# Forward to backward in a transformer block's decode kernel: the M products of head 30, the transposes of w3 and three weight loads are put in another place

## The chip, the core and the metric

The kernel runs on one core of a Trainium2 chip. A core has five engines that run side by side and wait for each other through semaphores: TensorE (PE, with its weight loads as PEld) multiplies matrices into PSUM, VectorE (DVE) and ScalarE (ACT) work element by element, GpSimd (POOL) and SyncE (SP) here issue transfers. Sixteen DMA engines move data between HBM and the on-chip memory. The metric is the device time of one execution in microseconds (us); lower is better. "Span" is the time from the first to the last instruction in the profiled execution.

## What is computed

One token goes through an adaptive-layer-norm block (attention over a cache of 8192 keys in 32 heads of width 192, then an MLP), and then the gradients of all inputs are formed. Cut to what matters:

```python
# B = 1, Sq = 1, D = 640, 32 heads, Sk = 8192, Dh = 192, F = 1536
def _A_ref(x, k, v, wq, wo):
    q = (x @ wq) as 32 heads
    p = softmax(einsum('bhqd,bhkd->bhqk', q, k) * Dh ** -0.5)
    return einsum('bhqk,bhkd->bhqd', p, v) as one row @ wo

def _B_ref(x, w1, w2, w3, w4):
    ...
    x1 = x + hs                      # hs is 0 for a single token
    return x1 + gelu(layernorm(x1) @ w3) @ w4

sa, ca, ga, sb, cb, gb = (silu(c) @ w_mod) in six parts
h = layernorm(x) * (1 + ca) + sa
x = x + ga * _A_ref(h, k_cache, v_cache, wq, wo)
h = layernorm(x) * (1 + cb) + sb
x = x + gb * _B_ref(h, w1, w2, w3, w4)
# returned: x, and the gradients of x, k_cache, v_cache, wq, wo, w3, w4, c and w_mod
```

The caches are 100.7 MB each; they are read, and their gradients (of the same size) are written.

## The kernel before

**Forward loop.** It runs over heads 0 to 30 (`for i in range(H1)`, H1 = 31) with three heads in flight: the scores of head i, softmax and scaling of V for head i−1, the end of head i−2. K and V come in halves of 1.57 MB (`load_k`, `load_v`) into five K buffers and three V buffers. Scores are products on DVE (`dot_mul`), summed by TensorE through the identity matrix. Each V half gives two quarters of V scaled by the exponentials ("vs", `scale_v`: some rows on DVE at L350, the others on ACT at L357, one ACTIVATE for each of up to 16 rows). For each quarter `m_quarter` adds K^T · vs to the head's matrix M (16 products at L372 for the first 128 columns of K, 16 at L377 for the other 64). M is kept, because the backward gets the gradient of q from it. The head's output row comes from a third set of products.

**The crossing.** After the loop comes straight-line code for the last two heads. Head 31 has no M; its output row, and that of head 30, come from `o_rows` (L392, 64 products each). Then: the output rows are divided by their sums (`pair_sums` L437 and L439, `pair_o` L443 to L448), multiplied with wo (`pair_ao` L455) and added into x1 (L651); layer norm 1, h_b, layer norm 2 (`g_layernorm`, a generator that is stepped with `next`, so that other work can be written between its steps; each mean is a product at L123); u = n2 · w3 (L783); gelu and its derivative; d_g, the gradient at the gelu's output, by twelve reductions of w4 on DVE (`dg_part`, L472); du; d_n2 from the transposed w3 (L834); two layer norms backward (`layernorm_bwd`); dao; and do, the gradient at the heads' outputs (`do_mm` L762, written to do_r at L765), the first operand of the backward loop.

Between these steps the code has other work: M of head 30 in quarters (`m_units` gives a quarter as three functions: the first 8 products of L372, the other 8, the 16 of L377; they are run by `f()` or `pe.pop(0)()`), the scaling of V for these quarters, the transposes of w3 (`w3t`, L725, with a copy from PSUM each, L726), gelu(u) · w4 (`h2_mm`, L822), the transposes of wo (`do_t`, L746), `mp_out` and `m_add` (M out of PSUM, L408, L410, L422), `e_rows` and `e_rows_out` (the exponentials transposed and stored to DRAM, L426 to L432; `load_er` at L704 loads them again for the backward).

**Loads of the crossing, in SP's order.** At i = 29 the loop issues three of w4's twelve row blocks into `w4b` (L560), at i = 30 the last pair's wo (L214), then the last V half of head 31, `load_v(H1, 1, KY)`. After it come the other nine blocks of w4 (L612), four fifths of w3 into the K buffer KX (L631) and the last fifth (L632).

**Backward loop.** It runs over 64 half heads. Each loads a V half, forms dP = V · do (L855 on DVE, L864 on PE, L314), dS, dK (L880) and dV (L875 on PE, L876 on ACT) and stores both; "side jobs" (weight gradients, q's gradient) are put between by a planner of slots.

**Order.** Within the crossing and the backward the order on PE, DVE, ACT and SP is that of the code (`manual_schedule`); POOL's order is that of its issues. Buffers come from pools: a tile is reused when its last reader is done, and where a pool is closed, its memory goes to later pools. The backward's pool `bst` is opened after the crossing's `vs` and `ft` are closed.

## Time and profile before

| | |
|---|---|
| times of the runs | 1434.04, 1435.51, 1438.58 us; median 1435.51 |
| the profiled execution | 1433.26 us, its span 1431.5 us |
| PE, DVE, ACT busy | 1105.0, 1104.2, 871.5 us (77%, 77%, 61% of the span) |
| moved | 569.38 MB by DMA; HBM read 340.95 MB, written 226.43 MB |
| mean granted TensorE clock | 0.768 |
| forward loop, crossing, backward | to about 533 us; 533 to about 594; from there to the end |

Busy shares are averages over stages with different limits. The page's slices divide the span into forty stretches of 35.8 us; a digit is a busy share in tenths, "PEclk" the TensorE clock that was granted (9 is full speed). In the rows in order of time the columns are: start in us, duration in us, engine and line, the operation, output and input tile, shapes and count; in brackets stands how long the engine had been idle before, and what ended that.

### The profile page before, as it was taken

The numbers are of one execution on the slowest core, as the hardware profiler recorded it, in microseconds if no ns is written. First come the engines' busy times: TensorE is split into PE (matmuls) and PEld (weight loads), VectorE is DVE, ScalarE is ACT, GpSimd is POOL, SyncE is SP. The second block draws the span as 40 slices with busy tenths as digits, with TensorE's granted clock in tenths as the row PEclk, the third lists the DMA queues.
The fourth block names the chain that finished last, engine by engine and source line by source line (L and its number), as shares of the span: only waits on it lengthen the run. The fifth ranks groups of instructions, "written<-read, shape, count | busy, mean of one in ns | idle before, by whom it ended". The sixth has DMA issues, their size and how long they took to land.

```text
span 1431.5 us, 30396 instructions
## 1 busy us (share of the span) xinstructions
PE 1105.0 (77%) x12744; PEld 790.1 (55%) x12744; DVE 1104.2 (77%) x1410; ACT 871.5 (61%) x1953; POOL 145.6 (10%) x254
## 2 busy tenths in 40 slices
PE   3988889999999998767757677677777777666864
...
PEclk9999999999999998766667575666655555556565
DMA  9999999999999995499999999999999999999998
GB/s 374 391 397 418 415 417 417 412 422 411 420 408 413 418 415 211 164 385 428 422 399 425 427 408 421 416 425 403 425 418 425 402 422 414 358 385 382 422 404 372
DMA packets 77417, 569.38 MB, mean 398 GB/s; under 512 B 8766, under 2 KB 26510, under 8 KB 36958
## 3 DMA queue, kind: packets, MB, share of 16 engines
...
q10 hardware_dynamic: 20, 0.00, 0.0%
HBM read 340.95 MB, written 226.43 MB: 396 GB/s over the span
## 4 chain that ended last, share of the span: by engine, by line
PE 26%; DVE 12%; DMA 8%; ACT 8%; issue 4%; POOL 1%; ACTq 0%; POOLq 0%; DVEq 0%; SPq 0%
PE dot_ps L864 17%; DVE pq L855 6%; ACT KB L876 6%; DMA wo_st<-in_A_wo_dram 4%; PE wT_ps L746 3%; PE dv_ps L875 3%; DMA stg<-in_A_wq_dram 2%; ACT wT L747 2%; DMA out_dram<-wo_st 2%; DVE dP L314 2%; DVE KB L880 1%; DMA out_dram<-stg 1%; PE do_ps L762 1%; DVE dq_junk L984 1%; DVE dS L1156 0%
## 5 line engine op out<-in xcount | busy, mean ns | idle before, releaser
L876 ACT CAST KB<-dv_ps 128x768 bf16<-128x768 f32 x512 | 376.3, 815 | 146.9 <-PE dv_ps L875 146.5
L864 PE MATMUL dot_ps<-pq,ident_bf 128*128 128x256 bf16 x1536 | 317.2, 388 | 50.2 <-DVE pq L855 50.1
L357 ACT ACTIVATE vs<-VB,Ef 128x192 bf16<-128x192 bf16 x872 | 314.9, 447 | 0.0
L864 PEld LDWEIGHTS <-ident_bf 128*128 128x128 bf16 x1536 | 198.5, 133 | 146.2 <-issue 77.4
L875 PE MATMUL dv_ps<-do_r,er_b 1*128 1x192 bf16 x2048 | 173.5, 309 | 131.1 <-ACT KB L876 129.9
L300 DVE TENSOR_TENSOR prod<-KB,qs_bc 128x6144 bf16<-128x6144 bf16 x62 | 207.9, 3353 | 30.0 <-DMA KB<-in_A_k_cache_dram 23.0
L880 DVE TENSOR_TENSOR KB<-qs_bc,dS 128x3072 bf16<-128x3072 bf16 x128 | 223.8, 1749 | 4.5 <-DMA out_dram<-KB 4.2
L855 DVE TENSOR_TENSOR pq<-VB,do_r 128x3072 bf16<-128x3072 bf16 x126 | 220.3, 1749 | 0.0
L372 PE MATMUL mp<-vs,KB 128*128 128x193 bf16 x1984 | 191.3, 249 | 4.3 <-ACT vs L357 2.8
L747 ACT COPY wT<-wT_ps 128x1024 bf16<-128x1024 bf16 x84 | 81.0, 964 | 185.4 <-PE wT_ps L746 185.4
L875 PEld LDWEIGHTS <-er_b 1*128 1x128 bf16 x2048 | 65.7, 102 | 223.2 <-issue 220.4
L372 PEld LDWEIGHTS <-KB 128*128 128x128 bf16 x1984 | 171.2, 98 | 13.6 <-DMA KB<-in_A_k_cache_dram 4.7
L310 PE MATMUL half_ps<-prod,ident_bf 128*128 128x256 bf16 x744 | 95.1, 279 | 45.8 <-DVE prod L304 45.4
L314 DVE TENSOR_REDUCE dP<-dot_ps 128x32 f32<-128x512 f32 x64 | 44.0, 688 | 109.8 <-PE dot_ps L864 109.8
L350 DVE TENSOR_TENSOR vs<-VB,E 128x1728 bf16<-128x1728 bf16 (+1 forms) x122 | 127.1, 1062 | 0.3 <-ACT vs L357 0.3
L304 DVE TENSOR_TENSOR prod<-prod 128x3072 bf16<-128x3072 bf16 x62 | 108.7, 1753 | 1.0
L310 PEld LDWEIGHTS <-ident_bf 128*128 128x128 bf16 x744 | 72.8, 99 | 64.1 <-issue 55.0
L377 PE MATMUL mp<-vs,KB 128*64 128x193 bf16 x1984 | 108.0, 252 | 0.0
L377 PEld LDWEIGHTS <-KB 128*64 128x64 bf16 x1984 | 80.8, 111 | 19.8 <-issue 19.7
L337 ACT ACTIVATE E<-S_h,negm 128x256 bf16<-128x256 f32 x31 | 15.8, 508 | 116.0 <-DVE negm L498 113.7
L704 POOL DMA_DIRECT2D er_b<-eT_d x64 | 37.3, 583 | 476.1 <-PE dv_ps L875 474.3
L432 POOL DMA_DIRECT2D eT_d<-er x16 | 8.8, 548 | 560.1 <-ACT vs L348 519.7
...
## 6 DMA issues: line engine op xcount, KB each, us to landing
...
VB<-in_A_v_cache_dram SPq DMA_DIRECT2D x123, 1536.0 KB, 11.6
...
```

Of the source, the lines that this page charges most:

```text
L300: V_.tensor_tensor(out=prod, in0=src, in1=vec[:, None, :].to_broadcast([P, JH, DH]), op=ALU.mult)
L310: T_.matmul(ps, lhsT=ident_bf, rhs=prod[:, :, k : k + TF], start=(k == 0), stop=(k == w - TF))
L350: V_.tensor_tensor(out=vs[:, 0:n, 0:DH].rearrange("p j (a b) -> p j a b", b=4), in0=v[:, v0 : v0 + n, :].rearrange("p j (a b) -> p j a b", ...
L357: A_.activation(out=vs[:, k, 0:DH], in_=v[:, v0 + k, :], func=ACT.Copy, scale=Ef[:, j0 + k : j0 + k + 1])
L372: T_.matmul(mp[:, 0:MW], lhsT=kb[:, j0 + k, 0:P], rhs=vs[:, k, 0:MW], start=(q == 0 and k == 0), stop=(z and k == JQ - 1), skip_group_chec ...
L377: T_.matmul(mp[p0 : p0 + 64, MO : MO + MW], lhsT=kb[:, j0 + k, P:DH], rhs=vs[:, k, 0:MW], start=False, stop=(z and k >= JQ - 2), skip_grou ...
L747: A_.copy(out=wT[:, x0 * P : (x0 + n) * P], in_=tp[:, 0 : n * P])
L855: V_.tensor_tensor(out=pq[:, q], in0=v_l[s][:, q * JQ : (q + 1) * JQ, :], in1=do_of(ht(s)[0])[:, None, :].to_broadcast([P, JQ, DH]), op=AL ...
L864: T_.matmul(ps[:, q * JQ : (q + 1) * JQ, :], lhsT=ident_bf, rhs=pq[:, q, :, k : k + TS], start=(k == 0), stop=(k == DH - TS), skip_group_c ...
L875: T_.matmul(ps[:, b, k * DH : (k + 1) * DH], lhsT=er[p0 : p0 + 1, 2 * m + k, :], rhs=doh[p0 : p0 + 1, :], start=True, stop=True)
L876: A_.copy(out=dV4[:, 2 * q : 2 * q + 2, m * PW : (m + 1) * PW], in_=ps[:, :, 0:PW])
L880: V_.tensor_tensor(out=dK[:, lo:hi, :].rearrange("p j (a b) -> p j a b", b=4), in0=qh.rearrange("p (a b) -> p a b", b=4)[:, None, :, :].to ...
```

## The change

In the loop, the loads of `w4b` at i = 29 and of the last wo at i = 30 go; both are issued after the last V half. In the crossing, the pair sums of heads 28 and 29 are taken ahead of head 30's V scaling; both `o_rows` follow each other; the four quarters of M are run in pieces of 8 or 16 products, each behind one of the chain's products on PE (quarter 0 around the output projection, quarter 1 in layer norm 1, quarter 2 in layer norm 2, quarter 3 among the transposes of w3). The scaling of quarters 0 and 2 is ACT's, that of 1 and 3 DVE's in halves of 8 rows (`vs_dve`). The last pair's o2 is made directly from the sums (`rm`). The large w3 load is issued behind quarter 1, which reads the buffer it goes to. `g_layernorm` can write a bf16 copy directly. w3's transposes, u, gelu, du, h2 and dn are moved into the crossing's pools: the transposes go to two `vs` buffers and KC in place of KC, `stg` and `w4b`, and use the PSUM of the score trees. The gelu's derivative is written with fewer steps behind the exponential. Both transposes of the last wo stand around dn and go to `w4b`; `mp_out` and `m_add` of head 30 come last.

(The lines of the crossing are indented less here than in the code.)

```diff
 def g_layernorm(x, name, res, n_bf=None):
...
+        if n_bf is not None:
+            V_.tensor_scalar(out=n_bf, in0=xc, scalar1=r[:, 0:1], scalar2=None, op0=ALU.mult)
...
-                if i % 2 == 0 and i > 0:
+                if i % 2 == 0 and 0 < i < H1 - 1:
                     wo_l[i // 2] = load_wo(i // 2)
...
-                if i == H1 - 2:
-                    nc.sync.dma_start(out=w4b[:, 0 : 3 * D].rearrange("p (a r) -> p a r", a=3), in_=w4v[:, 0:3, :])
...
+    def new_vs(q):
+        vs = vsp.tile([P, JQ, VW], BF16, name="vs")
+        A_.copy(out=vs[:, :, DH:VW], in_=E4[:, q * JQ : (q + 1) * JQ, :])
+        return vs
+    def vs_dve(vs, q, lo, hi):
+        j0, v0 = q * JQ, (q % 2) * JQ
+        V_.tensor_tensor(
+            out=vs[:, lo:hi, 0:DH].rearrange("p j (a b) -> p j a b", b=4),
+            in0=vy[q // 2][:, v0 + lo : v0 + hi, :].rearrange("p j (a b) -> p j a b", b=4),
+            in1=E4[:, j0 + lo : j0 + hi, None, :].to_broadcast([P, hi - lo, DH // 4, 4]),
+            op=ALU.mult,
+        )
+    def vs_act(vs, q, lo, hi):
+        j0, v0 = q * JQ, (q % 2) * JQ
+        for k in range(lo, hi):
+            A_.activation(out=vs[:, k, 0:DH], in_=vy[q // 2][:, v0 + k, :], func=ACT.Copy, scale=Ef[:, j0 + k : j0 + k + 1])
...
     x["v"].append(load_v(H1, 1, KY))
+    wo_l[TL] = load_wo(TL)
+    nc.sync.dma_start(out=w4b[:, 0 : 3 * D].rearrange("p (a r) -> p a r", a=3), in_=w4v[:, 0:3, :])
     negm = neg_max(mx)
     E4, Ef = softmax(H1 - 1, y["S"], negm)
     score_q(0, 1, d0)
     mt = m_out(H1 - 2, z["mp"], z["op"], os_)
-    op_y = psO.tile([P, 256], FP32, name="op")
-    o_rows(H1 - 1, vy, op_y)
-    vs0 = scale_v(0, vy[0], E4, Ef, 0)
-    mp = psM.tile([P, 512], FP32, name="mp")
+    po = pair_sums(os_.pop(TL - 1))
+    vs0 = new_vs(0)
+    vs_act(vs0, 0, 0, JQ)
     score_q(1, 0, d1)
     score_q(1, 1, d1)
-    vs1 = scale_v(1, vy[0], E4, Ef, JQ)
-    dot_sum(d0, x["S"][:, 0:JH])
-    for f in m_units(0, ky[0], vs0, mp):
-        f()
-    dot_sum(d1, x["S"][:, JH:J])
-    mx = row_max(x["S"])
-    po = pair_sums(os_.pop(TL - 1))
-    o_out(H1 - 1, op_y, os_)
     w4a = pp.tile([P, 9, D], BF16, name="w4a", tag="prod")
     nc.sync.dma_start(out=w4a, in_=w4v[:, 3:12, :])
     w4r = lambda a: w4b[:, a * D : (a + 1) * D] if a < 3 else w4a[:, a - 3, :]
-    for f in m_units(1, ky[0], vs1, mp):
-        f()
+    o2 = pair_o(TL - 1, po)
+    dot_sum(d0, x["S"][:, 0:JH])
+    mp = psM.tile([P, 512], FP32, name="mp")
+    pe = m_units(0, ky[0], vs0, mp)
+    pe.pop(0)()
+    dot_sum(d1, x["S"][:, JH:J])
+    mx = row_max(x["S"])
+    es0 = tcol(1, "es")
+    V_.reduce_sum(out=es0, in_=E_all[:, H1 - 1, :], axis=AX.X)
+    oy, zy = os_head(H1 - 1, os_)
+    ox, zx = os_head(H1, os_)
+    os2 = os_.pop(TL)
+    vs1 = new_vs(1)
+    A_.activation(out=zy, in_=es0, func=ACT.Copy, scale=32.0)
+    vs2 = new_vs(2)
     negm = neg_max(mx)
     A_.activation(out=E_all[:, H1, :], in_=x["S"], func=ACT.Exp, bias=negm[:, 0:1], scale=1.0)
+    op_y = psO.tile([P, 256], FP32, name="op")
+    o_rows(H1 - 1, vy, op_y)
+    vs_dve(vs1, 1, 0, JQ // 2)
+    es1 = tcol(1, "es")
+    V_.reduce_sum(out=es1, in_=E_all[:, H1, :], axis=AX.X)
+    vs_act(vs2, 2, 0, 1)
+    A_.activation(out=zx, in_=es1, func=ACT.Copy, scale=32.0)
+    A_.copy(out=oy, in_=op_y[:, 0:DH])
+    vs_dve(vs1, 1, JQ // 2, JQ)
     op_x = psO.tile([P, 256], FP32, name="op")
     o_rows(H1, x["v"], op_x)
-    vs2 = scale_v(2, vy[1], E4, Ef, JQ)
-    o2 = pair_o(TL - 1, po)
+    vs_act(vs2, 2, 1, 4)
     m_add(H1 - 2, z["mp"], mt)
-    vs3_ = []
-    vs3g = g_scale_v(3, vy[1], E4, Ef, vs3_, 0)
-    for _ in range(4):
-        next(vs3g)
-    ps_ao = pair_ao(o2, wo_l.pop(TL - 1))
-    V_.tensor_copy(out=AO[:, :, 2 * TL - 2 : 2 * TL], in_=ps_ao)
+    A_.copy(out=ox, in_=op_x[:, 0:DH])
+    ps_ao = pair_ao(o2, wo_l.pop(TL - 1), psB, "b")
     w3d = B_w3.rearrange("(i p) n -> p i n", p=P)
     w3_4 = wst.tile([P, F], BF16, name="w3_4", tag="wo")
-    nc.sync.dma_start(out=flat(KX)[:, 0 : 4 * F].rearrange("p (i n) -> p i n", i=4), in_=w3d[:, 0:4, :])
     nc.sync.dma_start(out=w3_4, in_=w3d[:, 4, :])
-    o_out(H1, op_x, os_)
+    po = psS.tile([P, 8], FP32, name="po", tag="s")
+    T_.matmul(po[:, 4:6], lhsT=c32, rhs=os2[:, 2 * DH : 2 * DH + 2], start=True, stop=True)
+    V_.tensor_copy(out=AO[:, :, 2 * TL - 2 : 2 * TL], in_=ps_ao)
+    V_.reciprocal(out=rinv[:, 2 * TL : 2 * TL + 2], in_=po[:, 4:6])
+    rm = tcol(2, "rm")
+    V_.tensor_tensor(out=rm, in0=omask[:, 0, :], in1=rinv[:, 2 * TL : 2 * TL + 2], op=ALU.mult)
+    for k in range(3):
+        T_.matmul(po[:, k : k + 1], lhsT=os2[:, k : 2 * DH : 3], rhs=c32[:, 0:1], start=True, stop=True)
+    vs_act(vs2, 2, 4, 8)
     aoP = tcol(ND, "aoP")
     V_.reduce_sum(out=aoP, in_=AO[:, :, 0 : 2 * TL], axis=AX.X)
     xP = tcol(ND, "xP")
     V_.tensor_tensor(out=xP, in0=ga, in1=aoP, op=ALU.mult)
     V_.tensor_tensor(out=xP, in0=xP, in1=x_c, op=ALU.add)
-    pe = m_units(2, ky[1], vs2, mp)
     pe.pop(0)()
-    po = pair_sums(os_.pop(TL))
-    dg_part(2)
-    o2 = pair_o(TL, po)
+    o2 = ft.tile([P, 3, 2], BF16, name="o2")
+    V_.tensor_tensor(out=o2, in0=po[:, 0:3, None].to_broadcast([P, 3, 2]), in1=rm[:, None, :].to_broadcast([P, 3, 2]), op=ALU.mult)
...
+    ps_ao = pair_ao(o2, wo_l[TL], psB, "b")
     pe.pop(0)()
-    ps_ao = pair_ao(o2, wo_l[TL], psB, "b")
-    for _ in vs3g:
-        pass
+    vs_act(vs2, 2, 8, JQ)
     aoN = tcol(ND, "aoN")
     V_.reduce_sum(out=aoN, in_=ps_ao, axis=AX.X)
     V_.tensor_tensor(out=x1, in0=ga, in1=aoN, op=ALU.mult)
...
     g = g_layernorm(x1, "ln1", res)
     next(g)
     V_.tensor_copy(out=AO[:, :, 2 * TL : 2 * TL + 2], in_=ps_ao)
+    pe = m_units(1, ky[0], vs1, mp)
     pe.pop(0)()
-    dg_part(1)
+    er_ps = e_rows(TL - 1, psB, "b")
     next(g)
-    pe = m_units(3, ky[1], vs3_[0], mp)
+    vs3 = new_vs(3)
+    vs_dve(vs3, 3, 0, JQ // 2)
     pe.pop(0)()
+    next(g)
+    e_rows_out(TL - 1, er_ps)
     pe.pop(0)()
-    dg_part(1)
-    next(g)
-    dg_part(1)
+    nc.sync.dma_start(out=flat(KX)[:, 0 : 4 * F].rearrange("p (i n) -> p i n", i=4), in_=w3d[:, 0:4, :])
+    vs_dve(vs3, 3, JQ // 2, JQ)
     next(g, None)
     n1, r1 = res.pop()
     V_.scalar_tensor_tensor(out=h_b, in0=cb, scalar=1.0, in1=n1, op0=ALU.add, op1=ALU.mult)
     V_.tensor_tensor(out=h_b, in0=h_b, in1=sb, op=ALU.add)
-    g2 = g_layernorm(h_b, "ln2", res)
-    next(g2)
-    pe.pop(0)()
-    dg_part(1)
-    mt = mp_out(H1 - 1, mp)
-    e_rows_out(TL - 1, e_rows(TL - 1, psB, "b"))
-    e_rows_out(TL, e_rows(TL, psB, "b"))
+    n2_bf = tcol(ND, "n2_bf", BF16)
+    g2 = g_layernorm(h_b, "ln2", res, n2_bf)
     next(g2)
     dg_part(1)
+    pe = m_units(2, ky[1], vs2, mp)
+    pe.pop(0)()
+    er_ps = e_rows(TL, psB, "b")
+    next(g2)
+    dg_part(1)
+    pe.pop(0)()
+    pe.pop(0)()
+    e_rows_out(TL, er_ps)
+    next(g2)
+    dg_part(1)
+    T0, T1 = (vsp.tile([P, JQ, VW], BF16, name="vs").rearrange("p j d -> p (j d)") for _ in range(2))
+    w3v = [flat(KX)[:, k * F : (k + 1) * F] for k in range(4)] + [w3_4]
+    w3Tv = [h[:, a * D : (a + 1) * D] for h in (T0, T1, flat(KC)) for a in range(4)]
+    def w3t_gen():
+        for a in range(NF):
+            tp = psR.tile([P, 1024], BF16, name="w3T_ps", tag="dot_ps")
+            for k in range(ND):
+                T_.transpose(out=tp[:, k * P : (k + 1) * P], in_=w3v[k][:, a * P : (a + 1) * P], identity=ident_bf)
+            A_.copy(out=w3Tv[a], in_=tp[:, 0:D])
+            yield
+    w3t_it = w3t_gen()
+    def w3t(n):
+        for _ in range(n):
+            next(w3t_it, None)
+    pe = m_units(3, ky[1], vs3, mp)
+    pe.pop(0)()
+    w3t(2)
+    next(g2, None)
+    n2, r2 = res.pop()
+    ups = psS.tile([P, NF], FP32, name="u_ps", tag="s")
+    for a in range(NF):
+        for k in range(ND):
+            T_.matmul(ups[:, a : a + 1], lhsT=w3v[k][:, a * P : (a + 1) * P], rhs=n2_bf[:, k : k + 1], start=(k == 0), stop=(k == ND - 1))
+    dg_part(2)
...
+    V_.tensor_copy(out=u, in_=ups)
+    V_.scalar_tensor_tensor(out=k2, in0=u, scalar=GELU_K1, in1=u, op0=ALU.mult, op1=ALU.mult)
+    V_.scalar_tensor_tensor(out=w_, in0=k2, scalar=1.0, in1=u, op0=ALU.add, op1=ALU.mult)
+    A_.activation(out=w_, in_=w_, func=ACT.Exp, scale=-2.0 * GELU_K0)
+    V_.tensor_scalar(out=e1, in0=k2, scalar1=6.0 * GELU_K0, scalar2=2.0 * GELU_K0, op0=ALU.mult, op1=ALU.add)
+    V_.tensor_tensor(out=e1, in0=e1, in1=u, op=ALU.mult)
+    w3t(2)
+    pe.pop(0)()
+    w3t(2)
+    pe.pop(0)()
+    V_.tensor_scalar(out=w_, in0=w_, scalar1=1.0, scalar2=None, op0=ALU.add)
+    V_.reciprocal(out=s_, in_=w_)
+    V_.tensor_tensor(out=g_, in0=s_, in1=u, op=ALU.mult)
+    g_bf = col(NF, "g_bf", BF16)
+    V_.tensor_copy(out=g_bf, in_=g_)
+    V_.scalar_tensor_tensor(out=t_, in0=s_, scalar=-1.0, in1=e1, op0=ALU.add, op1=ALU.mult)
+    V_.scalar_tensor_tensor(out=t_, in0=t_, scalar=-1.0, in1=s_, op0=ALU.add, op1=ALU.mult)
+    dg_part(NF)
+    du_bf = col(NF, "du_bf", BF16)
+    V_.scalar_tensor_tensor(out=du_bf, in0=t_, scalar=-1.0, in1=d_g, op0=ALU.mult, op1=ALU.mult)
+    V_.scalar_tensor_tensor(out=du, in0=t_, scalar=-1.0, in1=d_g, op0=ALU.mult, op1=ALU.mult)
...
+    w3t(2)
+    h2_mm(0, 2)
+    w3t(2)
+    h2_mm(2, 4)
+    w3t(2)
+    h2_mm(4, ND)
+    dw4_dve(flat(KX), 0, 0, 4)
...
+    def do_t(t, x0):
+        if x0 == 0:
+            woT[t] = w4b[:, 0 : 3 * D] if t == TL else bst.tile([P, 15 * P], BF16, name="wT", tag="wT")
+        w = wo_l[t]
+        transposed(x0, lambda a, b: [(0, P, w[:, a, b * P : (b + 1) * P])], 3, woT[t])
+    do_t(TL, 0)
+    dn_ps = psS.tile([P, ND], FP32, name="dn_ps", tag="s")
+    for k in range(ND):
+        for a in range(NF):
+            T_.matmul(dn_ps[:, k : k + 1], lhsT=w3Tv[a][:, k * P : (k + 1) * P], rhs=du_bf[:, a : a + 1], start=(a == 0), stop=(a == NF - 1))
+    d_n2 = tcol(ND, "d_n2")
+    V_.tensor_copy(out=d_n2, in_=dn_ps)
+    do_t(TL, 8)
+    mt = mp_out(H1 - 1, mp)
     m_add(H1 - 1, mp, mt)
...
-    w3Tv = [flat(KC)[:, a * D : (a + 1) * D] for a in range(9)] + [stg0[:, 0:D], stg0[:, D : 2 * D], w4b[:, 5 * D : 6 * D]]
...
-    w3t(1)()
-    next(g2)
-    dg_part(1)
-    next(g2, None)
-    n2, r2 = res.pop()
-    n2_bf = tcol(ND, "n2_bf", BF16)
-    V_.tensor_copy(out=n2_bf, in_=n2)
-    w3t(2)()
...
-    w3t(2)()
-    dg_part(2)
...
-    h2_mm(0, 2)
-    w3t(1)()
-    h2_mm(2, 4)
-    w3t(NF)()
-    h2_mm(4, ND)
-    dw4_dve(flat(KX), 0, 0, 4)
-    do_t(TL, 0)
-    dn_ps = psS.tile([P, ND], FP32, name="dn_ps", tag="s")
-    for k in range(ND):
-        for a in range(NF):
-            T_.matmul(dn_ps[:, k : k + 1], lhsT=w3Tv[a][:, k * P : (k + 1) * P], rhs=du_bf[:, a : a + 1], start=(a == 0), stop=(a == NF - 1))
     wo_l[TL - 1] = load_wo(TL - 1)
     er_l = {0: load_er(0), 1: load_er(1)}
-    d_n2 = tcol(ND, "d_n2")
-    V_.tensor_copy(out=d_n2, in_=dn_ps)
-    layernorm_bwd(d_n2, n2, r2, dbo, d_sb, "lb2", lambda: (do_t(TL, 8), dw4_dve(flat(KX), 0, 4, 5)))
+    layernorm_bwd(d_n2, n2, r2, dbo, d_sb, "lb2", lambda: dw4_dve(flat(KX), 0, 4, 5))
```

## The prediction

> **What bounds the kernel now.** I read the page's slices first, then one table of stretches, then the rows in order of time around the crossing from forward to backward.
>
> ```profile
> PE   3988889999999998767757677677777777666864
> PEclk9999999999999998766667575666655555556565
> DMA  9999999999999995499999999999999999999998
> GB/s 374 391 397 418 415 417 417 412 422 411 420 408 413 418 415 211 164 385 428 422 399 425 427 408 421 416 425 403 425 418 425 402 422 414 358 385 382 422 404 372
> ```
>
> Transfers fill both halves. They thin out only in slices 15 and 16 (537 to 608 us): 211 and 164 GB/s against some 415. There nothing is left to load and nothing is ready to store, so a chain of small steps sets the time, and a microsecond cut from it starts the whole backward a microsecond earlier.
>
> ```profile
> core 0: us, PE busy (x) PEld busy (x) DVE busy (x) ACT busy (x) POOL busy (x), PEclk, DMA share, GB/s
> 546.00:550.00 4.00, 4.00 (x48) 3.69 (x46) 3.06 (x8) 0.92 (x6) 0.00 (x0) 1.00 0.92 303
> 554.00:558.00 4.00, 2.61 (x32) 2.40 (x32) 3.21 (x14) 4.00 (x12) 0.00 (x0) 0.96 0.99 392
> 558.00:562.00 4.00, 4.00 (x32) 3.58 (x33) 3.28 (x14) 0.60 (x3) 0.00 (x0) 0.50 0.03 10
> 574.00:578.00 4.00, 4.00 (x87) 4.00 (x85) 1.61 (x6) 2.69 (x5) 0.00 (x0) 0.50 0.07 10
> ```
>
> Columns: window, its length, busy time per engine, granted clock, DMA share, GB/s. DMA is idle from 558 on, the TensorE clock is halved from there, and no engine is busy throughout: it is latency. The links, in order:
>
> ```profile
> 540.33 3.43 DVE L570 TENSOR_TENSOR pb<-KB,qs_bc 128x3072 bf16<-128x3072 bf16 x2 [3.09 <-DMA KB<-in_A_k_cache_dram]
> 543.68 1.75 DVE L350 TENSOR_TENSOR vs<-VB,E 128x3072 bf16<-128x3072 bf16 x1
> 549.08 0.20 ACT L404 ACTIVATE osb<-es 128x1 f32<-128x1 f32 x1 [3.28 <-PE po L439]
> 549.39 0.35 ACT L617 ACTIVATE E_all<-S_h,negm 128x64 bf16<-128x64 f32 x1
> 551.19 0.38 SPq L631 DMA_DIRECT2D KB<-in_B_w_dram  x1
> 554.04 0.82 DVE L472 CUSTOM_DVE_ANT_0 w4b<-w4b 128x640 bf16<-128x640 bf16 x1
> 557.51 0.17 DVE L651 TENSOR_TENSOR x<-x,xP 128x5 f32<-128x5 f32 x1
> 567.93 0.17 DVE L778 CAST n_bf<-ln_n 128x5 bf16<-128x5 f32 x1
> 569.93 0.17 DVE L788 COPY u<-u_ps 128x12 f32<-128x12 f32 x1 [0.23 <-PE u_ps L783]
> 574.10 0.17 DVE L808 CAST du_bf<-du 128x12 bf16<-128x12 f32 x1
> 579.66 0.16 DVE L839 COPY d_n<-dn_ps 128x5 f32<-128x5 f32 x1 [2.50 <-PE dn_ps L834]
> 585.26 0.42 ACT L765 ACTIVATE do_r<-do_ps,rinv 128x192 bf16<-128x192 f32 x1 [2.75 <-PE do_ps L762]
> ```
>
> The last K half lands at 540.33; the last exponential is at 549.39, x1 at 557.51, the second layer norm at 567.93, u at 569.93, du at 574.10, d_n2 at 579.66, the backward's first operand do_r at 585.26: 45 us in which little is moved.
>
> **The change, step by step.** Each line gives the end of a link before, and worked out for after.
>
> *Loads.* wo (0.49 MB) and the first part of w4 (0.49 MB) go behind V. The queue is full there; wo's landing followed K's by 1.16 us (540.21, 541.37), so K lands about 1.2 earlier (539.1), and the last half of V, 2.4 earlier, near 546.5. SP only issues in another order, nothing is queued behind a new wait.
>
> *Scores to exponential.* Before, both score sums stood behind the 1.75 us scaling at 543.68, and ACT waited until 549.08 for L439, queued on PE behind 16+16 M products. Both leave. What remains: two products 3.43, tree 1.47, sum 0.69, maximum 0.22, mx 0.49, negm 0.29, exponential 0.35, seven hand-overs at 0.04: 7.2. It ends at 546.3 instead of 549.74. Gain 3.4.
>
> *Output rows to x1.* Two L392 groups of 64 (1.50 each) run back to back, the second on V at 546.5: end 548.8 instead of 552.59. Then copy 0.30, sums 0.38 and 1.18, o2 0.17, ao 0.51, three DVE steps 0.6, hand-overs 0.3: 3.4. Before it was 5.1, with two L472 reductions (0.86 from start to start) ahead of o2. x1 ends at 552.3 instead of 557.68. Gain 5.4.
>
> *Two layer norms.* On PE an M block of 8 (half of L372's 1.51 per 16: 0.75 to 0.84) now stands behind each link, where whole quarters stood at half clock (2.75 and 1.50). A block of 8 lies beside the small DVE and ACT steps (0.7), the rest of 16 (0.86) beside Ln, Exp and what follows. Chain of the two: four means at 0.56, their sums 0.16, and 0.23+0.17, 0.29+0.20, 0.23 twice, h_b 0.34, hand-overs: 6.9. n2 at 559.2 instead of 568.10. The four half scalings of 1536 are not in the trace: at most 1.05 (L350 at 1728 columns), at least 0.84 (half of 1.68 back to back); 0.95 taken, in DVE's gaps. The second er copy waits on ACT for the first one's store (before: 3.45 from issue to landing) ahead of Ln: up to 1 us, hidden by the next step.
>
> *w3, the new wait.* Its 1.57 MB are issued behind the rest of M quarter 1, at 555.9 instead of 551.19. L214 at 576.90, alone on the queue, took 3.3 for 0.49 MB, of which 1.16 is transfer: 2.1 fixed. w3 then takes 2.1+3.7 = 5.8, bounds 3.7 (nothing fixed) and 9.8 (the V loads' median in this stretch under load); the queue is empty, so 5.8, landing 561.7. The link waits 2.5 for it. Ten transposes 0.7, 60 u products 1.74, copy: u at 564.4 instead of 570.1. Gain 5.7.
>
> *gelu and the w4 reductions.* Of twelve L472 only five are done by then; seven follow at 0.86: 6.0 after 2.0 of gelu steps, so du_bf is at 572.4 instead of 574.27. DVE has become the end here; beside it ACT needs 12 copies at 0.69 = 8.3 from 562.3 on (571 to 573), and PE its transposes, 24 M products and h2 (8 to 9 us at full clock). The four gelu steps saved (0.2 each) hide under this. Gain 1.9.
>
> *dn.* Before, PE came to dn 3.6 after du, held by transposes and h2 (577.83). Now these lie beside the seven reductions: dn 572.8 to 574.7, d_n2 4.9 earlier.
>
> *To do_r.* The layer norms' backward stays, 4.5. m_add (0.35) and its wait for two ACT copies (0.64), behind two wT copies (1.01 and 0.91), now stand between them on DVE: 0.4, at most 1.0. er's loads wait for that m_add: issued at 577.3 instead of 572.28, 1.9 to land, 579.2 against do_r at 580.6: 1.4 of cover, and PE's first dv_groups, c_ps and tree queue behind it if it goes.
>
> Sum: 4.9 − 0.4 = 4.5 us earlier. The backward does the same work behind it, so the shift carries to the end. Against this execution's own 1433.26 (span 1431.5 and 1.8 around it): 1428.8. It lies 2.25 below the median of the runs shown, 1435.51, which gives 1431.0 as the median to expect.
>
> **The clock.** The grant comes in steps of 3.4 us at 1.00 or 0.50: 0.96 over 554 to 558, where PE was busy 2.61 of 4 us, then 0.50. The sum has full clock up to w3's wait and a mix after.
> [...]
>
> **Rivals.**
> 1. *Half clock from w3's wait to the end of dn* (chance 0.17). For it: transposes and one-column products at 574 to 578 kept PE busy 4.00 of 4 us at 0.50. Then PE's work after u (five groups of ten transposes at 1.42, 8 M 1.37, 16 rest 1.50, h2 1.5) is 11.5 instead of 8: h2 ends at 576 only, less what overlaps u. Gain some 3.0: 1432.5.
> 2. *Full clock throughout* (0.10). The c_ps group 2.27, the tree 2.56 (1.47 at full) and do_mm 1.00 (0.59 later) lose 1.1, 1.1 and 0.4, dn and means 1: gain some 8: 1427.5. Against it: one-column products and a 2.5 us wait in the middle.
> 3. *Slower: the halving comes with the thin M blocks, before 551* (0.13). Dense M quarters (4.00 of 4 us at 546 to 550) are what is spread out; if a 3.4 us stretch there falls short, each 8-block costs 0.53 more and each rest 0.64: five and three of them on the path give 4.5. w3 is issued 2.5 later (its share), u ends at 567.5, PE's 12 us end at 579.5, dn at 581.5 against 579.63, with m_add 2.4 slower: 1437.9. It decides if 0.50 is granted ahead of 551. Against it: o rows are dense just then.
> 4. *The gain isn't kept* (0.10): the backward's buffers and 3.4 us clock steps regroup its waits (chain rows PE dot_ps 17%, DMA wo_st 4%), as runs of one kernel differ by 4.5 us: about 1435.
>
> **Numbers.** The forecast, gain 4.5 (2 to 7), has 0.50. What a measurement can tell from no change here is about 0.3%, 4.3 us: the forecast lies at that bound. Faster: 0.5·0.6 + 0.17·0.3 + 0.10 + some of 4 = 0.48. Slower: 0.13·0.6 of the third, 0.03 of the fourth, 0.04 of covers lost (er, w3 at 9.8): 0.15. Within: 0.37. Range 1426.0 to 1437.5: below it lie the best of rival 2, above it the worst of rival 3; the forecast's own is 1428.5 to 1433.5.
>
> **What would show it.** The exponential ending 3.4 earlier and x1 5.4 earlier; a wait of about 2.5 us of PE for w3's load ahead of its transposes; seven L472 in a row ahead of du; PE idle before dn on DVE, not the reverse; do_r near 580.8. It is wrong if PE has the half clock before w3's wait, if w3 lands after 563, if dv_groups waits for er, or if do_r is early and the end is not.

## The result: slower, and the profile after

The median went from 1434.1 us (10 runs, 1433.0 to 1438.6) to 1440.62 us (10 runs, 1437.1 to 1444.8): ratio 1.0042, 95% interval 1.0029 to 1.0056. The profiled execution after took 1439.51 us, its span is 1437.7 us (before: 1433.26 and 1431.5).

First the page of the kernel after: the slices of 36 us and, from its part 3, the queue that brings instructions.

```profile
PEclk8999999999999998566655666565655656657556
DMA  9999999999999994589999999999999999999998
GB/s 375 399 419 418 416 415 416 410 420 415 412 416 418 416 397 169 201 317 428 425 390 423 426 416 425 424 424 395 425 416 422 397 424 399 364 391 380 414 412 369
...
q8 instruction: 100, 1.64, 0.5%
```

Slices 15 to 17 are still thin, and in slice 17 (611 to 647 us) 317 GB/s stand where before had 385: the backward's start is poorer, not the crossing alone. The clock is 0.5 in slice 16 (575 to 611 us), where before had 0.7.

The same table of stretches of the kernel after (window, length, busy time per engine, granted clock, DMA share, GB/s):

```profile
546.00:550.00 4.00, 1.58 (x61) 1.34 (x51) 1.74 (x8) 4.00 (x13) 0.00 (x0) 0.95 1.06 357
550.00:554.00 4.00, 3.94 (x41) 3.84 (x43) 1.09 (x7) 1.41 (x5) 0.00 (x0) 0.50 0.21 75
558.00:562.00 4.00, 3.55 (x49) 2.90 (x44) 3.90 (x15) 0.76 (x3) 1.00 (x2) 1.00 0.66 201
562.00:566.00 4.00, 1.70 (x45) 1.47 (x43) 1.07 (x4) 0.83 (x2) 0.00 (x0) 1.00 0.54 213
574.00:578.00 4.00, 3.84 (x97) 3.66 (x94) 2.98 (x13) 2.49 (x4) 0.00 (x0) 0.86 0.43 127
586.00:594.00 8.00, 8.00 (x49) 5.23 (x48) 3.27 (x10) 2.36 (x4) 1.39 (x2) 0.50 0.71 267
594.00:602.00 8.00, 6.83 (x47) 4.11 (x48) 6.75 (x5) 2.46 (x4) 1.67 (x3) 0.50 0.35 108
602.00:610.00 8.00, 6.92 (x76) 4.61 (x68) 3.55 (x6) 3.43 (x6) 0.00 (x0) 0.50 0.99 377
```

PE is busy for only 1.58 us of the first stretch, where the plan was dense; then the clock is 0.50. It recovers for the layer norms and the w3 wait, and is 0.50 without a break from 586 to 610. The links, from the timeline (start, duration, engine, line, operation):

```profile
537.66 3.43 DVE L570 TENSOR_TENSOR pb<-KB,qs_bc 128x3072 bf16<-128x3072 bf16 x2 [2.92 <-DMA KB<-in_A_k_cache_dram]
544.50 0.35 ACT L642 ACTIVATE E_all<-S_h,negm 128x64 bf16<-128x64 f32 x1 [0.33 <-DVE negm L583]
553.64 0.17 DVE L687 TENSOR_TENSOR x<-x,xP 128x5 f32<-128x5 f32 x1
558.24 0.37 SPq L702 DMA_DIRECT2D KB<-in_B_w_dram  x1
561.14 0.23 DVE L155 TENSOR_SCALAR n_bf<-ln_xc,ln_r 128x5 bf16<-128x5 f32 x1
566.94 0.17 DVE L751 COPY u<-u_ps 128x12 f32<-128x12 f32 x1 [3.84 <-PE u_ps L748]
574.91 0.17 DVE L770 SCALAR_TENSOR_TENSOR du_bf<-t__10310,d_g 128x12 bf16<-128x12 f32 x1
577.04 0.17 DVE L821 COPY d_n<-dn_ps 128x5 f32<-128x5 f32 x1 [0.69 <-PE dn_ps L819]
583.11 0.42 ACT L876 ACTIVATE do_r<-do_ps,rinv 128x192 bf16<-128x192 f32 x1 [3.84 <-PE do_ps L873]
```

do_r ends at 583.5 instead of 585.7, 2.2 earlier, and yet the end is 6.2 later. Cut at four points (the start of the products with the last K half, the end of the last exponential, of do_r, and dP of the fourth half head of the backward), with the time the clock stood at 0.50 in the last but one stretch:

```
         last K  K->exp  exp->do_r  do_r->dP4  dP4->end   end    0.50 in do_r->dP4
before   540.3    9.4      35.9       41.2      804.6    1431.5     13.9 us
after    537.7    7.2      38.7       48.6      805.6    1437.7     44.5 us
change   -2.6    -2.2      +2.8       +7.4      +1.0      +6.2
```

Two stretches lost: exp to do_r, the part that was rebuilt, and do_r to dP4, which the diff doesn't touch. The other 60 half heads take nearly the same time (1.0 us more).

**Exp to do_r.** The waits of PE in the kernel after, 540 to 604 us (total, times, longest), and PE's rows around the first of them:

```profile
PE po L668 <- issue: 2.5, 1, 2.5
PE w3T_ps L730 <- DMA KB<-in_B_w_dram: 2.3, 1, 2.3
```

```profile
544.07 2.16 PE L394 MATMUL op<-VB,E_all 128*32 128x192 bf16 x96
546.06 0.83 PE L394 MATMUL op<-KB,E_all 128*32 128x192 bf16 x32
546.83 0.53 PE L457 MATMUL ao_ps<-o,wo_st 128*128 128x2 bf16 x15
547.22 0.36 PE L662 MATMUL po<-osb,c 128*128 128x2 f32 x2
550.06 1.44 PE L668 MATMUL po<-c,osb 128*128 128x1 f32 x6 [2.48 <-issue]
```

The second wait is the forecast one. The first has no releaser: PE stood for 2.48 us with nothing that the profile shows to wait for. The instruction queue's row gives the clue: 100 packets of 16,384 bytes beside 25,488 products and weight loads on PE, some 255 to a packet; as the records of this trace place them, PE's code came in blocks of 256 instructions. PE entered a block at 544.4; the two `o_rows` groups back to back (128 products, each a weight load and a matmul) used it up by 547.6; the packet with the next block had started only at 547.4, 3.0 us behind the entry (the DMA engines are full there, 1.06), and PE went on 5.7 us after the entry. Before, the same kind of block was entered at 541.9, its follower's packet ran at 545.1, and it wasn't needed until 551.6. This is an inference from the order in time; the first experiment tests it.

**Do_r to dP4.** The score trees of the backward, first of the kernel after, then of the kernel before (timeline, PE):

```profile
586.49 2.75 PE L910 MATMUL dot_ps<-pq,ident_bf 128*128 128x256 bf16 x12
589.92 2.74 PE L910 MATMUL dot_ps<-pq,ident_bf 128*128 128x256 bf16 x12
595.51 2.74 PE L910 MATMUL dot_ps<-pq,ident_bf 128*128 128x256 bf16 x12 [1.17 <-DVE pq L901]
```

```profile
588.63 2.75 PE L864 MATMUL dot_ps<-pq,ident_bf 128*128 128x256 bf16 x12
591.98 1.48 PE L864 MATMUL dot_ps<-pq,ident_bf 128*128 128x256 bf16 x12
596.31 1.48 PE L864 MATMUL dot_ps<-pq,ident_bf 128*128 128x256 bf16 x12 [1.89 <-DVE pq L855]
```

Same products, 2.74 against 1.48 us. Before, the clock rises behind the first tree and stays up for a while; after, it doesn't rise until 617.8.

### The profile page after: what moved, and what is told of

Same layout as the page of the kernel before. It is cut to its first block, busy times and chain, and to the rows that moved or that the text cites. A ratio compares the mean times of both kernels' runs of the same rounds, so it can differ in the third digit from the quotient of the medians.

```text
span 1437.7 us, 30394 instructions
## 1 busy us (share of the span) xinstructions
PE 1116.1 (78%) x12744; PEld 792.4 (55%) x12744; DVE 1103.8 (77%) x1411; ACT 871.8 (61%) x1953; POOL 145.5 (10%) x254
## 4 chain that ended last, share of the span: by engine, by line
PE 26%; DVE 10%; ACT 9%; DMA 9%; issue 5%; POOL 1%; ACTq 0%; POOLq 0%; SPq 0%; DVEq 0%
PE dot_ps L910 17%; ACT KB L922 6%; DVE pq L901 5%; PE wT_ps L804 3%; PE dv_ps L921 3%; DMA out_dram<-wo_st 3%; DMA stg<-in_A_wq_dram 2%; ACT wT L805 2%; DMA wo_st<-in_A_wo_dram 2%; DMA er_b<-eT_d 1%; DVE KB L926 1%; DVE dP L316 1%; DMA out_dram<-KB 1%; DVE dq_junk L1030 1%; PE do_ps L873 1%
## 5 line engine op out<-in xcount | busy, mean ns | idle before, releaser
L910 PE MATMUL dot_ps<-pq,ident_bf 128*128 128x256 bf16 x1536 | 326.2, 396 | 49.1 <-DVE pq L901 48.8
L359 ACT ACTIVATE vs<-VB,Ef 128x192 bf16<-128x192 bf16 x840 | 303.8, 448 | 0.0
L910 PEld LDWEIGHTS <-ident_bf 128*128 128x128 bf16 x1536 | 202.5, 136 | 150.8 <-issue 78.8
L921 PE MATMUL dv_ps<-do_r,er_b 1*128 1x192 bf16 x2048 | 177.3, 315 | 133.5 <-ACT KB L922 128.1
L374 PEld LDWEIGHTS <-KB 128*128 128x128 bf16 x1984 | 170.1, 98 | 13.9 <-DMA KB<-in_A_k_cache_dram 5.9
L312 PE MATMUL half_ps<-prod,ident_bf 128*128 128x256 bf16 x744 | 95.1, 279 | 43.7 <-DVE prod L306 43.3
L352 DVE TENSOR_TENSOR vs<-VB,E 128x1728 bf16<-128x1728 bf16 x120 | 123.7, 1051 | 0.3 <-ACT vs L359 0.3
L312 PEld LDWEIGHTS <-ident_bf 128*128 128x128 bf16 x744 | 73.0, 99 | 62.1 <-issue 52.9
```

Of the source, the lines that this page charges most:

```text
L312: T_.matmul(ps, lhsT=ident_bf, rhs=prod[:, :, k : k + TF], start=(k == 0), stop=(k == w - TF))
L352: V_.tensor_tensor(out=vs[:, 0:n, 0:DH].rearrange("p j (a b) -> p j a b", b=4), in0=v[:, v0 : v0 + n, :].rearrange("p j (a b) -> p j a b", ...
L359: A_.activation(out=vs[:, k, 0:DH], in_=v[:, v0 + k, :], func=ACT.Copy, scale=Ef[:, j0 + k : j0 + k + 1])
L374: T_.matmul(mp[:, 0:MW], lhsT=kb[:, j0 + k, 0:P], rhs=vs[:, k, 0:MW], start=(q == 0 and k == 0), stop=(z and k == JQ - 1), skip_group_chec ...
L910: T_.matmul(ps[:, q * JQ : (q + 1) * JQ, :], lhsT=ident_bf, rhs=pq[:, q, :, k : k + TS], start=(k == 0), stop=(k == DH - TS), skip_group_c ...
L921: T_.matmul(ps[:, b, k * DH : (k + 1) * DH], lhsT=er[p0 : p0 + 1, 2 * m + k, :], rhs=doh[p0 : p0 + 1, :], start=True, stop=True)
```

## The experiments

All medians with the ratio to the kernel before on the same chip, as it is on record (12 runs each, unless said); it is not the quotient of two medians, and medians of different rows can be from different chips. The stretches are of one profile for each kernel, in us; the last column is the time at clock 0.50 in do_r to dP4. A profile is of one execution and need not be a typical one: those of e2, e11, e14 and e18 are of the slowest of their timed runs, those of e6 and e16 of the fastest.

```
                        median   ratio [95%]              last K  K->exp exp->do_r do_r->dP4  0.50
e1_code_shift           1435.72  1.0016 [0.9998, 1.0033]   536.8   8.1    35.3      47.1      36.9
e2_warm                 1439.98  1.0046 [1.0025, 1.0068]   542.2   8.5    40.6      48.1      40.7
e3_warm_onerow          1438.24  1.0038 [1.0022, 1.0054]   541.0   7.5    41.6      44.8      31.1
e4_shift_warm           1434.07  1.0003 [0.9985, 1.0022]   538.3   7.2    35.9      43.7      26.6
e5_shift_trees          1440.78  1.0047 [1.0026, 1.0069]   538.4   7.9    37.7      51.6      27.7
e6_before_trees         1439.76  1.0049 [1.0027, 1.0071]   538.1   9.4    34.1      49.8      25.9
e7_before_again         1432.83  one run                   538.6   9.4    36.0      41.3      14.0
e8_shift_entry          1432.00  0.9996 [0.9984, 1.0008]   540.0   7.2    38.0      43.7      23.2
e9_before_entry         1436.58  1.0014 [0.9997, 1.0031]   537.9   9.4    34.2      47.2      36.3
e10_shift_entry_early   1433.97  1.0004 [0.9989, 1.0019]   538.7   7.3    37.8      44.2      27.1
e11_dense (7 runs)      1430.64  0.9951 [0.9934, 0.9969]   541.1   7.6    33.8      47.1      36.4
e12_dense_madd          1434.04  0.9992 [0.9978, 1.0005]   537.8   8.4    36.2      47.1      36.1
e13_shift_delay         1425.89  0.9940 [0.9922, 0.9958]   531.0   7.8    37.7      48.6      44.5
e14_before_delay        1440.00  1.0030 [1.0010, 1.0049]   539.0   9.4    37.1      48.7      45.0
e15_dense_again         1431.15  0.9981 [0.9963, 0.9999]   536.9   8.1    34.5      43.6      23.1
e16_before_align (6)    1427.46  0.9952 [0.9933, 0.9970]   532.3   9.4    32.7      41.4      14.0
e17_dense_align         1431.88  0.9985 [0.9969, 1.0001]   535.9   7.8    33.9      47.0      36.1
e18_shift_align         1436.49  1.0022 [1.0004, 1.0041]   538.3   7.8    38.2      48.6      44.7
```

**Is the gap PE's code?** 144 cheap PE instructions where PE waits for the first K anyway (15 to 20 us) move every later block boundary; nothing in the crossing changes.

```diff
+            cps = psB.tile([P, 512], FP32, name="code_ps", tag="b")
+            for _ in range(72):
+                T_.matmul(cps[:, 0:1], lhsT=ident_bf, rhs=ident_bf[:, 0:1], start=True, stop=True)
```

> The changed kernel with 72 one-column products more on PE at about 15 to 20 us, where PE waits for the first K half; nothing else. They shift the place of every later PE instruction in its code by 144 instructions. Theory A (PE ran out of code): the trace of the changed kernel has a PE gap of 2.5 us ahead of L668 that nothing releases, and the transfer of the next 16 KB of PE's code, every 256 PE instructions, starts only at 547.4, 3.0 us after PE entered the block before it; the two o_rows back to back use up a whole block in 2.7 us. With the shift no block ahead of 575 takes under 7 us, so the gap goes: L668 follows the exponential as before, the granted clock is 1.00 in 550 to 554, w3 is issued near 555.9, do_r ends near 581, and the end is 2 to 3 us earlier, 1438. Rival (the gap is a wait of L668 itself, for a buffer or for ACT): the gap stays ahead of L668, do_r stays at 583.1 and the time at 1440.6.

The same rows of e1_code_shift (timeline, PE):

```profile
547.20 0.36 PE L665 MATMUL po<-osb,c 128*128 128x2 f32 x2
547.92 1.18 PE L671 MATMUL po<-c,osb 128*128 128x1 f32 x6 [0.35 <-DVE rinv L667]
548.96 0.84 PE L374 MATMUL mp<-vs,KB 128*128 128x193 bf16 x8
```

The gap is gone, PE waits 0.35 us for the reciprocal that the code names, and x1 ends 5.9 us behind the exponential instead of 9.0. L668 and what it reads are the same, so the rival (a wait of L668 itself) is out. The median falls by 4.9 us, or 4.4 where each kernel is set against the kernel before on its own chip. The gap of about 2.5 us stood in each of the three profiles without the shift (after, e2, e3) and in none of the eleven shifted ones. Not all of the 4.9 need be the gap itself: in this profile the clock also held longer, until 561.5.

**Can dummy products keep the clock up into the backward?** 4, 8 and 6 products of 256 columns with no use behind h2 and in the two layer norms' backward; e3 the same with one row of the array (`ident_bf[0:1]`, `dbo_bc[0:1]`; in before at clock 1.00 a product of 192 columns with one row, L875, takes 238 to 252 ns, one of 193 with 128 rows, L372, 244 to 257); e4 is e2 with the shift.

```diff
+                    T_.matmul(h2_ps[:, 256:512], lhsT=ident_bf[0:P, :], rhs=dbo_bc[0:P, 0:256], start=True, stop=True)
```

> The changed kernel with 18 extra products of 128x128 by 256 columns on PE, written beside h2's columns and read by nobody: 4 behind h2, 8 and 6 while PE waits for DVE in the two layer norms backward. Theory B (the lost time behind do_r is the half clock at the entry of the backward, 0.50 from 577 to 618): the clock stays at 1.00 for most of 577 to 600, the first trees of the backward take 1.48 instead of 2.74 us, dP of the fourth half head comes 4 to 6 us earlier (632 before, 626 to 628 here) and the end is near 1435, some 5 earlier, although the 4 products ahead of dn cost up to 0.4. Rival C (the backward loses because of what the change moved: er loads behind m_add, woT in w4b, the loads' order): the first four half heads take 39 us whatever the clock, and the time stays within 1.5 of 1440.6.

> As the run with the 18 extra products, but each has one row of contraction instead of 128, so PE is busy for as long and does 1/128 of the work. In the two traces so far the clock was raised only behind 3.4 us windows of which products with 128 rows filled 0.73 or more, and fell behind windows with under 0.4; the one-row products of dV counted nothing. By that the clock stays at 0.50 from 577 on as in the changed kernel and the time is 1440 to 1442. Rival (any PE activity counts): the same as with 128 rows, clock 1.00 and some 1435.

> Both edits together: 72 one-column products early, and the 18 extra products of 128 rows. If A and B are separate and both right, do_r ends near 581, the first four half heads take some 33 us and the end is 7 to 8 earlier than the changed kernel's 1440.6: about 1432.5, just under the kernel before. If only A: 1438; only B: 1435; neither: 1440.6.

Stretches of e2_warm, then one of e3_warm_onerow:

```profile
578.00:582.00 4.00, 3.85 (x94) 3.56 (x91) 3.83 (x11) 2.94 (x6) 0.00 (x0) 0.97 0.01 4
586.00:590.00 4.00, 1.58 (x14) 0.97 (x11) 2.52 (x13) 0.57 (x3) 1.14 (x2) 1.00 0.02 4
590.00:594.00 4.00, 3.19 (x24) 2.90 (x25) 3.80 (x9) 1.92 (x3) 1.06 (x1) 0.74 0.23 84
```

```profile
582.00:586.00 4.00, 3.75 (x21) 2.62 (x19) 2.13 (x12) 1.45 (x3) 1.02 (x2) 0.50 0.00 0
```

Full rows hold the clock at 1.00 until 591.9, just past do_r (591.3), one row doesn't (0.50 from 581.6). But in e2 it falls again before the first tree, and do_r to dP4 is 48.1: the filler held the clock and bought nothing. With the shift (e4) the time is that of the kernel before.

**Do longer trees raise it?** Six more products with a zero matrix in each tree of the first six half heads, on after with the shift and on before.

```diff
+            if k == 0 and n_tree[0] <= 12:
+                for _ in range(6):
+                    T_.matmul(ps[:, q * JQ : (q + 1) * JQ, :], lhsT=zero_bf, rhs=pq[:, q, :, 0:TS], start=False, stop=False, skip_group_check=True)
```

> The changed kernel with the 72 early products (so without the gap ahead of L668), and in the first six half heads of the backward six more products with a zero matrix in each sum of 12 (L910's tree: 18 instead of 12, the sums unchanged). Theory B2: over the six profiled kernels so far the time from do_r to dP of the fourth half head is 37.8 us plus 0.245 for each us at half clock (13.9 to 44.5 us of it); at half clock a tree fills 2.56 us, which is 0.75 of a 3.41 us window, the very share from which the clock was raised, so a tree raises it only by chance. With 18 products (3.84 us at half clock, 1.92 at full) nearly every tree raises it: under 15 us of half clock, 41 to 42 us to the fourth dP instead of 47.1, and the end some 5 earlier than with the shift alone (1435.7): about 1431. Rival C (the entry is slow for what the change moved, not for the clock): 47 us again, and the 6 products more per tree cost 1 to 3 us: 1437 to 1438.

> The kernel before with the same 18-product trees in the first six half heads. If the kernel before is hit by the half clock at the entry as often as the changed one (B2, its profile with 13.9 us at half clock was a lucky one), it gains 2 to 5 from its 1433.6: 1429 to 1431. If its own entry is mostly at full clock, it gains nothing or loses up to 2: 1433 to 1436, and the question is what in the change takes the clock away.

> The kernel before once more, for a second profile. Lucky first profile: 44 to 48 us from do_r to the fourth dP with over 30 us at half clock. Entry mostly at full clock: 40 to 42 us with 10 to 20 at half clock, as in the first.

In e5 the half clock shrinks (27.7 against 36.9 in e1), but the added products cost more than it gives: 51.6 us. On before they cost as well (49.8 instead of 41.2), with more time at half clock besides (25.9 instead of 13.9). e7, the kernel before again, shows 41.3 and 14.0 us where its first profile had 41.2 and 13.9, though its forward ended 1.7 us earlier. Two like profiles don't show that each execution of before has this value; what they share is told in the section on the prediction.

**Two trees side by side.** Both first trees directly behind each other, so that one 3.4 us step of the clock has more of their products in it; e8 on after with the shift, e9 on before.

```diff
-    tree_q(ps, 0)
     mul_q(0, 1)
     dv_groups(dV0, er, do_of(H1), (4, 6))
+    tree_q(ps, 0)
+    tree_q(ps, 1)
...
-    tree_q(ps, 1)
```

> The changed kernel with the 72 early products, and the two first trees of the backward (12 products each) run back to back on PE behind both groups of dV instead of one on each side of the second group: the same instructions in another order, and the second tree ends no later. At half clock one tree fills 2.56 of a 3.41 us window, 0.75, and trees one dV group apart come every 3.4 us, so a window that cuts the first cuts the second too. Two in a row fill 5.1 us, so that one window always holds 0.75 or more. Theory B2: the clock is raised within 8 us of do_r in the profile, under 25 us at half clock to the fourth dP (36.9 with the shift alone), 41 to 44 us instead of 47.1, and the median 2 to 4 below 1435.7. Rival (the raise does not hold, since at full clock a tree is only 0.38 of a window, at the share of 0.37 under which it fell): raised and lost again, 46 us, 1435.

> The kernel before with the same reordering of its first two trees. Its two profiles were raised by the first tree at once (13.9 and 14.0 us at half clock). If that is how it mostly runs, nothing is gained: 1432 to 1434.5. If these were lucky, it gains 2 or more: under 1431.5.

Stretches of e8_shift_entry:

```profile
550.00:554.00 4.00, 3.76 (x43) 3.71 (x45) 1.90 (x12) 3.72 (x11) 0.00 (x0) 0.68 0.76 255
594.00:602.00 8.00, 4.69 (x77) 3.51 (x76) 7.93 (x8) 3.16 (x6) 1.64 (x3) 1.00 0.33 95
```

The entry runs at 1.00 from 594 to 602, where after had 0.50, and do_r to dP4 is 43.7. Before gets worse by the same edit (47.2). So the order isn't good or bad by itself. The first row shows the other loss: without the gap the clock still falls at 551.4, and exp to do_r is 38.0.

**Earlier reductions and m_add.** `dg_part(4)` instead of `dg_part(2)` in the w3 wait, and `mp_out` and `m_add` ahead of du instead of behind dn (e10 on e8, e12 the second alone on e11).

> As the run with shift and reordered trees, and in the crossing two more of the w4 reductions (0.86 each) in DVE's idle time while PE waits for w3, and M of head 30 copied and added before dn instead of between dn and d_n1. Seven reductions behind gelu become five: du 1.7 earlier, unless the twelve copies of w3's transposes on ACT (0.645 each) end it; m_add's 0.4 leaves the path. do_r 1 to 2 us earlier against the exponential (34 instead of 35.3), the median 1 to 2 below that run's, at best 1431 and under the kernel before. Rival (ACT's copies set dn): 0.4 only.

> As the run with M's blocks one place earlier, and M of head 30 taken out of PSUM behind w3's last transpose and added on DVE before dn's copy, so that m_add no longer stands between dmod and d_n1. d_n2 to do_r 0.4 shorter (5.9 instead of 6.3), the median within 1 of the other, no loss.

du came 1.8 sooner in e10, but dn still began only with the end of ACT's last copy of w3's transposes (du to d_n2 4.2 instead of 2.2): no gain. In e12 exp to do_r got longer (36.2 against e11's 33.8); no run shows why.

**M blocks dense again.** Quarter 0's second 8 products directly behind `o_rows`, its 16 behind the pair sums, quarter 1's first 8 behind ao, ao of heads 28 and 29 ahead of the maximum, w3 one place earlier; with the shift and the order of e8. e15 is the same kernel again.

```diff
             o_rows(H1, x["v"], op_x)
+            pe.pop(0)()
...
             ps_ao = pair_ao(o2, wo_l[TL], psB, "b")
+            pe = m_units(1, ky[0], vs1, mp)
             pe.pop(0)()
```

> The run with shift and reordered trees, and M's blocks one place earlier in the crossing: the second 8 products of quarter 0 directly behind the two o_rows, its 16 behind the pair sums, quarter 1's first 8 behind the output projection, and the projection of heads 28 and 29 (15 thin products) ahead of the maximum. In that run, and in the one with 18-product trees, PE had 2.9 us of thin products behind the o_rows, and the clock fell to 0.50 at 551 although the 2.5 us gap was gone: x1 to n2 8.1, exponential to do_r 38.0 and 37.7 us, against 35.3 where the halving came at 561. Theory D (thin products halve the clock in the M blocks, rival 3 of the prediction): with dense blocks between, no drop before 556, w3 issued within 5 us of x1's end less than before (x1 + 3), exponential to do_r 34.5 to 35.5 and the median 1 to 3 under that run's 1432: 1429 to 1431. Rival (the blocks ahead of the sums only delay x1): x1 0.5 to 1 later, do_r the same, 1432 to 1433.

> The version with shift, reordered trees and denser blocks once more, for more timed runs: 1429 to 1432, 2 to 4 under the kernel before on the same chip.

A stretch of e11_dense:

```profile
550.00:554.00 4.00, 3.65 (x72) 3.27 (x63) 1.84 (x10) 4.00 (x13) 0.00 (x0) 1.00 0.92 325
```

The clock is 1.00 where after had 0.50 and e8 0.68, and exp to do_r is 33.8 and 34.5, where the forecast's sum gives 34.9 (do_r's end 585.7, less its 4.5, less 546.3). Both runs are faster than before, e15 barely; e12 and e17, which are this version with one edit more, are not told from before (0.9992, 0.9985). The first four half heads of e11 and e15 differ (47.1, 43.6): in the same kernel the clock of the entry came out differently.

**Is it the place in time?** A chain of dependent copies of 5 columns ahead of `dao_bf` that only delays do_r: 7 (some 1.4 us) on after with the shift, 8 (1.65 us) on before.

```diff
+    for k in range(8):
+        dm = col(ND, f"dl{k}")
+        V_.tensor_copy(out=dm, in_=dl)
+        dl = dm
```

> The changed kernel with the 72 early products, and seven copies of five columns on DVE in a row ahead of dao_bf, some 1.4 us in which nothing else is done: do_r comes 1.4 later against everything ahead of it. If the changed kernel stands to the clock windows in a fixed way (a window beginning 0.2 to 1.9 us behind do_r, where no tree fits), the delay moves the next one to 2.2 to 3.4, the first tree fits in many runs and the kernel is faster by being later: 1433 to 1434.5 against 1435.7 with the shift alone. If the place is chance, it is slower by the delay: 1437.

> The kernel before with eight such copies, 1.65 us. If its place (a window 2.7 to 2.9 us behind do_r) is fixed, it becomes 1.1 to 1.3, the first two trees miss, and it loses the delay and 3 to 5 more: 1438 to 1440, with 44 us or more from do_r to the fourth dP. If it is chance, the delay alone: 1435.5.

The same two stretches of the kernel before, then of e14_before_delay, the kernel before's own work done 1.65 us later:

```profile
594.00:602.00 8.00, 4.70 (x77) 3.53 (x76) 7.93 (x8) 3.22 (x6) 1.88 (x4) 1.00 0.44 141
602.00:610.00 8.00, 5.11 (x65) 3.51 (x58) 6.00 (x7) 6.63 (x10) 0.35 (x2) 0.93 0.99 364
```

```profile
594.00:602.00 8.00, 6.83 (x43) 4.01 (x41) 7.28 (x6) 3.12 (x5) 0.72 (x2) 0.50 0.37 121
602.00:610.00 8.00, 6.93 (x68) 4.29 (x67) 3.16 (x4) 3.43 (x6) 1.07 (x2) 0.50 0.91 333
```

e14's rows are the changed kernel's in PE's busy time and clock, with 45.0 us at half clock and 48.7 us to dP4: in this profile a delay of 1.65 us costs the kernel before 7.5 more in the entry. Its median is 1440.0 beside 1434.8 for the kernel before on the same chip; the interval of the ratio, some 1.4 to 7.0 us, does not exclude the bare 1.65, and three of its twelve runs (1431.8, 1432.1, 1434.0) are no slower than before. Its eight small constants move the later buffers by 256 bytes, so the place of these against multiples of 256, which matters below, is before's. In e13 the entry went from e1's 47.1 to 48.6, yet the run was the fastest of all: its last K half came at 531.0. Its seven constants had moved the later buffers by 224 bytes.

**Where the buffers lie.** One unused constant of 32 bytes per partition, on before, e11 and e1.

```diff
+    const.tile([P, 8], FP32, name="pad")
```

> The kernel before with one unused tile of 32 bytes per partition, so that all K, V, prod and weight buffers move from 32 to 0 modulo 64. If the address is the cause, the half heads of the forward come 0.14 us faster each, the last K lands near 531 instead of 539, and the time is 8 to 11 under the kernel before: 1424 to 1427. If it was something else: 1433 to 1436.

> The version with shift, reordered trees and denser blocks, with the same 32 bytes. If the two add: 8 to 10 under that version's 1431: 1421 to 1423.5, and 2 to 4 under the kernel before with 32 bytes.

> The changed kernel with the 72 early products and the same 32 bytes, without the delay. If the address explains the run with the delay, 1425 to 1428; the difference to that run's 1425.9 is then what the delay is worth: 1.4 slower there if the place in the clock windows is chance, up to 3 faster if the delay helped.

Only e16 gained: e17 is not told from the kernel before, and e18 is slower than it, so the 32 bytes don't add to the other edits. What the three share and don't is in the last section.

## Why the prediction was wrong, step by step

The forecast was a median of 1431.0 us, 4.5 faster in a range of 1426.0 to 1437.5; measured were 1440.6, 6.5 slower.

What held, after against the forecast: the scores to the exponential take 7.2 us (7.2). Exponential to x1, forecast 6.0, is 5.9 in e1; w3 is waited for 2.3 (2.5) and takes 6.4 from issue to use (5.8), so it costs no more than said; u to du 8.0 (8.0), with five reductions ahead of u and seven behind gelu; du to d_n2 2.1 (2.3); d_n2 to do_r 6.3 (5.9 before, and 0.4 for m_add). er's loads were issued at 580.2 and nobody waited for them. Two terms were off by less: the two layer norms took 7.6 (7.9 in e1) instead of 6.9, and dn began not behind du on DVE but with the end of ACT's last copy of w3's transposes, 0.3 us behind du (1.3 in e1). Three of the four signs of being wrong came: the half clock ahead of w3's wait, w3 in use only at 564.7, and do_r early without the end. The steps that failed are these:

1. **"K lands about 1.2 earlier"** isn't seen. The last K half began at 537.9 to 540.3 in the five profiles of before with its buffers in place (mean 538.8), at 535.9 to 542.2 in the thirteen changed ones (538.7).
2. **The output rows, "end 548.8"**: the products ran in less than the time given (2.8 us for both groups, 1.50 each) but used up their code faster than it came (the next packet started 3.0 us behind the entry into the block). The gap put x1 9.0 us behind the exponential instead of the sum's 6.0, and without it the median is 4.9 us lower (e1), or 4.1 where the clock falls early all the same (e18). A step that packs PE's instructions has one more supply to check; the sum put it at nothing without a word.
3. **"The sum has full clock up to w3's wait"** failed; rival 3 had the place and its test, 0.50 ahead of 551. It came at 549.6, behind a step with 2.0 of the gap's 2.48 us in it. Its ground "o rows are dense just then" was undone by the gap, but e8, e10 and e18 have no gap and fall at about 551 as well: exp to do_r 37.8 to 38.2, against 35.3 where it held until 561.5 (e1). So its price is 2.5 to 2.9 us, and not the 4.5 of the working. e18 is e1 with 32 bytes more, so the same code can go either way. In the four profiles with denser blocks (e11, e12, e15, e17) it held until 555.7 to 563.9. Rival 1's half clock from the w3 wait on didn't come (1.00 from 558 to 566, 0.58 and 0.99 behind), nor rival 2's full clock throughout, which no run shows (after had 0.50 from 549.6, 566.6 and 576.9).
4. **"The backward does the same work behind it, so the shift carries to the end"** is the step that decided between the two profiles. Same work, but not the same clock: 44.5 us at 0.50 instead of 13.9. Over the eighteen profiles without the longer trees, do_r to dP4 is 37.8 us plus 0.246 per us at half clock, with no residual over 0.7; so 30.6 us more at half clock are 7.5 us, the 7.4 measured, and nothing else that the change moved costs the entry more than 0.7. Rival 4 named the place ("3.4 us clock steps regroup its waits") but priced it at the spread of runs. e14 shows it alone: nothing but a delay, and its profile loses the same.

How much of the median's 6.5 us is this step's, one profile for each kernel can't tell: e1 takes 4.4 to 4.9 off by curing the second step (in the profiles 3.4 of it in exp to do_r and 1.5 in the entry), and what is left, about 2 us slower than before (its interval includes no change) where 4.5 faster was forecast, stands beside an entry of 47.1 us in its profile.

How the grant went with PE's products can be read from the traces. For each step of 3.413 us I added up the products' columns at the granted clock, weighted with the share of the array's rows and columns in use, and looked at the grant of the next step. Over 20 profiles (some 8230 steps; the counts move by a few per cent with how a product is placed in time):

```
at 0.50   share below 0.65: raised   0 of some 2300     0.65-0.75: 90 of some 490     0.75-0.80: 430 of some 490     over 0.80: all of some 600
at 1.00   share below 0.35: held     0 of some 1090     0.35-0.40: 105 of some 150    over 0.40: all of some 3100
```

In before and after alone (823 steps) the seven counts are 0 of 249, 10 of 51, 41 of 45 and all of 52, then 0 of 97, 12 of 20 and all of 309. Without the weight the same steps don't part: at 0.50 with a share over 0.80 only 96 of 298 are raised.

The loss in M's blocks and that of the entry both fit these counts. Thin blocks give the step 0.34 (e5, e8, e10, e18), the gap 0.17 (after), and the clock fell; e1 had 0.42 there and held, before 0.60. A tree is 12 times 256 columns, at half clock 0.213 us each from start to start (after and before; 1.2 columns per ns), so 2.56 us or 0.75 of a step, just where the counts turn. Before's step from 588.4 holds the whole first tree (0.76), and the next is at 1.00. After's first two trees come 3.43 us apart, the length of a step, so a tree that straddles the border of two steps is followed by another that does, and by this sum the parts in one step stay a hair under 0.75: 0.749 in the steps from 587.1 and 590.5, and the next of each is at 0.50.

Where the border fell can be read too, as the time from do_r's end to the next border. It goes with the half clock of the entry, whichever kernel it is (the fifteen profiles without filler products and longer trees):

```
first trees    border behind do_r    at 0.50 in do_r->dP4    profiles
apart          0.1 to 0.6            44.5 to 45.0            after, e13, e14, e18
apart          1.8                   36.9                    e1
apart          2.7 to 3.0            13.9 to 14.0            before, e7, e16
together       0.3 to 0.4            23.1 to 23.2            e8, e15
together       1.1                   27.1                    e10
together       1.9 to 2.2            36.1 to 36.4            e9, e11, e12, e17
```

e9 and e14 are the kernel before with one edit, and they stand with the changed kernels; e11 and e15, the same kernel, differ as their borders do. So the entry loses by where the border falls, not by what the change moved there. The borders showed no fixed place against the program: in each profile all changes of the grant lie on one grid of 3.4133 us, to 0.001 us from the first to the last, and the grid began 0.0 to 3.2 us, modulo a step, behind the first instruction (before 1.33, after 0.02). If the border's place is drawn anew in each execution, before's good entry and after's bad one were luck. Yet the five profiles of before without a delay have the border 2.1 to 3.0 us behind do_r (e6 and e9 at 2.1 and 2.2), the changed kernels 0.1 to 2.2. Whether that nearness is chance, or whether the chain, whose speed the clock sets, is drawn to one place of the grid, stays open.

## What to carry to other kernels

A shorter chain ahead of a loop is a gain only if the loop starts in the same state: look at the granted clock in the first iterations, and test the sum with a kernel that does nothing but delay the loop. One profile for each kernel shows one place of the clock's steps; a difference of a few us between two profiles can be that alone (the entries of e11 and e15, the same kernel: 47.1 and 43.6). Where TensorE's work is spread behind other links, keep the products of each 3.4 us together and with all rows and columns of the array: in the counts above every step over 0.40 held the clock, and some 430 of 490 at 0.75 to 0.80 and all over 0.80 raised it. An idle stretch of PE with no releaser, where some hundred small products run back to back under full queues, can be its code: here 2.48 us behind 128 products, gone when 144 idle instructions moved the block borders, and one run tells it.

## What the runs showed that had not been expected

**Where a buffer starts.** e13 and e16 had a faster forward, growing by some 0.1 us with each K half, and 7.7 and 6.5 us at its end against the mean of the changed kernels and of before. The stretches 100 to 200 and 400 to 500 of e7 (before), then of e16 (before and 32 bytes):

```profile
100.00:200.00 100.00, 89.09 (x1407) 75.53 (x1408) 91.79 (x88) 73.95 (x243) 1.63 (x3) 1.00 1.01 414
400.00:500.00 100.00, 91.45 (x1404) 76.83 (x1400) 94.14 (x91) 75.21 (x244) 1.62 (x3) 1.00 1.01 417
```

```profile
100.00:200.00 100.00, 91.06 (x1448) 76.99 (x1446) 93.73 (x91) 74.59 (x244) 1.62 (x3) 1.00 1.01 424
400.00:500.00 100.00, 93.57 (x1425) 78.65 (x1422) 95.75 (x93) 76.95 (x252) 1.61 (x3) 1.00 1.01 423
```

The DMA engines are full in both (1.01), but move 414 and 417 or 424 and 423 GB/s. In these two kernels the K and V buffers start at a multiple of 256 bytes in a partition (the first V buffer at 94208 and 93952). The others start 32, 64 or 224 bytes past one; 64 (e17 and e18, at 94016) gave nothing beyond the usual spread (61st K half at 512.8 and 515.1, others 513.3 to 517.5, the two fast ones 507.8), so a multiple of 64 isn't enough; 128 wasn't tried. One unused constant is worth 0.9952 [0.9933, 0.9970] on the kernel before, as much as anything else in this study. That the address is the cause rests on these two kernels. What such an address changes in a transfer, no run shows. The dense version together with such an address was not tried.

**The supply of code.** In before and after 100 packets of 16,384 bytes came beside 25,488 products and weight loads, so one for some 256 PE instructions; under full queues (200 to 540 us of both) it started some 2 us behind the entry into the block before it, 0.6 at the least and 3.9 at the most, and in the profile of after PE could go on only 5.7 us behind that entry where it had to wait.
